# Keeping DMA transposes, accumulating DMAs and GpSimd pieces apart in a list-scheduled attention kernel

## Chip, cores, metric

One core of one Trainium2 chip. The metric is the device time of one execution in microseconds (us). Every execution of the kernels that is used here was in the fast state; three of before's (858.6, 858.9 and 860.4 us) were in the slow one and are left out. The single run of the measuring program m1 has no state. Each execution also comes with the mean clock that TensorE was granted, as a share of full speed; that number turns out to matter.

## The reference, cut to what matters

```python
# S = 2048, D = 512, H = 32 heads, Dh = 16; bf16 inputs
g = sigmoid((x * gate_w).sum(-1, keepdims=True))
a = softmax(q @ k.T * Dh**-0.5) @ v           # per head, then @ wo        (branch A)
phi(t) = concat(softmax(t @ w_phi), softmax(-t @ w_phi))                 # (branch B)
b = phi(q) @ (phi(k).T @ v) / (phi(q) @ phi(k).sum(s) + 1e-6)            # then @ wo
return g * a + (1 - g) * b
```

Branch A costs 32 x 2048 x 2048 exponentials. They are the bulk of the work.

## The kernel before

A Python program lists all operations with their dependencies. A list scheduler simulates the engines with assumed durations and fixes the order of every engine's instructions; `place` then turns dependencies and buffer reuse into semaphore waits. So a number in the scheduler ("plan value") changes the order on the chip, and an assumed duration that is wrong makes the chip's timing drift from the plan.

The parts that matter here, in short:

- TensorE computes scores into PSUM, ScalarE takes the exponential (832 operations of 128x1024), TensorE multiplies by V.
- 96 score tiles get their exponential from VectorE and GpSimd instead. VectorE converts scores to integers (EW). GpSimd, sometimes VectorE, splits them into a fraction Ef and an exponent ED. VectorE evaluates a polynomial (Em, then Ef again). Then GpSimd issues an **accumulating DMA** ED += Ef, and a TensorE matmul reads ED.
- Branch B needs **DMA transposes** issued by SyncE: 48 of phi (128x1024) and 16 of the output (128x512).
- TensorE's busy time contains matmuls that only add zeros (`ps_ot<-zero,iden`: 110.0 us in before, 121.1 us in after). The scheduler puts them where its plan leaves TensorE idle, so a wait that the plan did not foresee has none of them.

```python
# 96 times: the accumulating DMA and its reader
v = s.op("pool", SWD[0], lambda e: e.dma_start(
    out().bitcast(dt.int16), Ef().bitcast(dt.int16), accum_op=ALU.add), [g_] + hs, pr, frees=[ef], dma=SWD[1])
v.kind = "acc"
...
return s.op("pe", 0.2155, ..., deps=vs + [self.o_V[(kt, part)]], ..., frees=[ed])

# 48 times: the transpose of phi
ev = self.s.op("sp", 1.3, lambda e: e.dma_start_transpose(
    self.phiT[:, pt.idx], self.phi[:, ph.idx].rearrange("p h s f -> p (h s f)")), deps, prio,
    alloc=[pt], frees=frees, dma=1)
ev.lat = 2.6
ev.kind = "phi"

# Sched.run: the port that VectorE and GpSimd share, and the landing of a DMA, as the plan saw them
if o.port:
    other = "dve" if e == "pool" else "pool"
    now = max(now, hold[other])
    hold[e] = now + o.dur
...
if o.dma > 1:
    dma_t = max(dma_t, o.end) + o.dma / 250e3
    o.end = dma_t + o.lat
else:
    o.end += o.lat
```

The plan models the shared port but does not enforce it; it knows nothing of two DMAs slowing each other.

The softmax here doesn't subtract the row's maximum and nothing guards it: scores larger than these inputs give would overflow.

Of the kernel before, what the change touches and what calls it, by code (L numbers as in the profile page):

```python
# [31 lines left out]
LEAD = [30.0, 5.0, 15.587634343078882, 18.596008015614277, 21.376333972175523, 40.540151693083416, 4.700229106743385, 13.0]  # L32
PACE = [0.942023613127232, 0.45790104673263465]
BOUNDS = [3.0710501327799653, 8.000889564597248, 8.0295624987611, 18.02257936663145, 29.86797202712817]
# [4 lines left out]
AFF = [4.15497164884861, 0.18343314021531576, 3.4899946808590343, 0.0, 0.0, 2.90437474412157, 0.0, 3.2417994652524023, 0.0, 0.04936235801504704, 0.5936669881661917, 0.48380220117050143, 0.0, 3.63018746007737, 3.491920909382754, 0.0, 2.1406325166983535, 0.0, 0.21204954920410735, 2.3328020332964208, 0.0, 0.22787943080925754, 0.0, 0.0, 0.7354200939583246, 0.0, 0.0, 0.0, 3.722000841705053, 0.0, 0.0, 0.0, 0.0]  # L39
PAIR = [0] * 33  # L40
JOINT = [0, 0, 1, 1, 1, 1, 0, 0, 0, 1, 0, 0, 1, 1, 0, 0, 0, 0, 0, 0, 1, 0, 0, 1, 0, 0, 0, 0, 0, 0, 1, 0, 0]
SWD = [0.65, 662500, 1.85]
OFF = [0.0, -0.8897703043510494, 0.5172481291637241, -1.6001482920023302, 2.691800625687394, -4.61876105583856, 9.931835604720934, 3.749480399812751, -2.5354011754586376, 6.457003779301287, 7.051784018513548, -6.13598057955875, 6.241188808437798, -6.3176738336357, -4.720084637924602, 5.808771137792029, 1.4939627059612288, 11.762173704833385, -7.056266514883313, 1.602535412833622, -2.1339281934554815, 6.8960641134545035, -1.5364304379614095, -4.520043988488846, -1.9086060678527623, 4.191789611328016, 0.0, -10.92683283831524, 7.908073056639142, -2.846662271061698, 1.1690496888958446, 2.378092297094616, 0.0]
PRI = [-2.5977761809841518, 12.575398704445774, 3.895376356683779, 7.787259417549168, -8.651933190709245, 8.964622677949125, 0.4457880973056989, 12.368950578623885, 19.409552720225648, -3.2493945476953874, -5.057883055897609, 4.784017942556362, 8.536057932420114, 2.626494246393886, 12.999207097537264, -0.8374814899478146, -17.665801839387232, -7.161052481135956, -12.903739516547825, 10.87669422388445, 2.941617488397717, -4.250877620548464, 10.157188453890655, -20.005512559792166, -9.773812266304459, 1.8583573414742158, -5.94449476159381, -2.8717857218875027, -7.6958394115627495, -2.7824756511447886, -12.357333215935258, 8.557379841186394, 0.0]
SHY = [0.9001243968886534, 1.4809346778702634, 0.0, 1.4435036371133614, 0.2648245103916662, 0.9580856445374635, 0.0, 0.0, 0.6445455027631356, 0.7309428588090539, 1.1375351044326518, 2.3433455863822243, 0.7756902927692249, 0.0, 0.5, 1.1003534700919317, 3.2731939951157525, 0.6932697202707927, 0.0, 1.9277987030895938, 0.6784790768552428, 0.0, 0.8699058379080198, 0.16347116433726255, 0.7631355271096165, 0.1372776832486249, 1.130856988716154, 3.243248686223888, 0.0, 0.5743497984785182, 0.26482053971962666, 0.0, 0.5]
FILL = [0.5, 0.8711172814468358, 0.09241059669762763, 0.6175020065897155, 0.5968855613401888, -0.08603643695579696, 0.35836419719938023, 0.5586945605907905, 0.5, 0.21748892677719284, 0.45750545023833894, 0.5973287974855181, 0.8575217902838435, 0.3303883794680146, 0.23663805939196605, -0.05074327763890446, 0.2084505307424424, 0.7627302738218456, 0.02798645175032277, 0.6920770580745201, 0.07174908565670901, 0.784881042335597, 0.9386617589290094, 0.3031481489097715, 0.2677360487923325, 0.24925630002968974, 0.3016740589041108, -0.013731781829222231, 0.4009774331892926, 0.4360673208434442, 0.33279011555474275, 0.6155190493677356, 0.5]
SLIP = [0.007477558429250707, 0.013771949294956619, 0.06040700872331797, 0.005290126503821307, 0.0, 0.04422179282875663, 0.0, 0.0, 0.0, 0.07161288987940874, 0.0, 0.0, 0.004963247503648168, 0.03943355056146375, 0.0, 0.002957841477534724, 0.0, 0.0, 0.06406254955060428, 0.009649379279412312, 0.06237810720540699, 0.07310479040093273, 0.037191229424563266, 0.03425975512431642, 0.0, 0.0924937571943965, 0.02436668932101764, 0.015526190087033388, 0.0417233434314886, 0.0764626104914441, 0.12735071923751323, 0.12964507975379921, 0.0]
POLY = [2.5698857428809108, -0.7915744377372271, 3.711634300285815, 3.2368110322825703, -2.325206997995846, 5.4861275628456045, -1.2275371530929335, 2.3718927004339707, 2.3718927004339707, 6.413096867619973, 5.17610762451314, -0.08970465716275755, 4.7841112088256725, 2.774473851459849, -2.7397699965795126, 1.9545390919678927, -1.3153066215108966, 1.617483163920298, 6.204660286247156, 5.766200947445682, 4.7687278506630655, -3.064800512746859, 7.929141786271487, 0.22420426790201642, 2.5526418134024933, 2.3718927004339707, -4.71404655949348, -1.3350112925734097, -2.638697537980217, -1.2887908683802543, 5.121320728096021, 2.3718927004339707, 2.3718927004339707]
SHAPE = [0, 1, 2, 2, 2, 1, 1, 2, 2, 2, 0, 0, 0, 1, 2, 0, 2, 0, 0, 0, 1, 1, 1, 0, 1, 0, 1, 1, 1, 1, 1, 1, 1]
# [11 lines left out]
DVE_COUNT = (1, 3, 3, 3, 3, 3, 3, 3, 1, 3, 4, 3, 3, 3, 3, 3, 3, 3, 4, 2, 4, 3, 3, 3, 3, 3, 4, 3, 4, 3, 3, 3)  # L61
# [22 lines left out]
class BufPool:  # L84
    def __init__(self, n):
        self.free = [(0.0, i, ()) for i in range(n)]
        self.parked = []
        self.want = None

# [32 lines left out]
class Sched:  # L122
# [18 lines left out]
    def op(self, eng, dur, fns, deps=(), prio=0.0, rel=0.0, alloc=(), frees=(), dma=0, order=(),  # L141
           cols=0, cfg="F", port=False, gate=False, alt=0.0):
        if not isinstance(fns, (list, tuple)):
            fns = [fns]
        if eng == "pe" and not cols:
            cols = 90
        o = Op(eng, dur, list(fns), deps, prio, rel, alloc, frees, dma, order, cols, cfg, port, gate, alt)
        if eng == "dve" and any(getattr(b.pool, "scarce", False) for b in o.frees):
            o.prio -= LEAD[2]
        self.ops.append(o)  # L150
        return o
# [34 lines left out]
    def run(self):  # L186
# [6 lines left out]
        t = {e: 0.75 for e in self.ENGS}  # L193
# [3 lines left out]
        out = []  # L197
        cfg = "F"
        hold = {"dve": 0.0, "pool": 0.0}
        parked, last = [], None  # L200
        self.at = 0
# [26 lines left out]
        while left:  # L228
# [43 lines left out]
            held, o = [], None  # L272
# [46 lines left out]
            for it in held:  # L319
                heapq.heappush(ready[e], it)  # L320
            ok = True
            for b in o.alloc:
                if b.idx is not None:
                    continue
                pool = b.pool
                pool.free.sort()
                need = sum(x.pool is pool and x.idx is None for x in o.alloc)
                w = pool.want
                if len(pool.free) < need or (
                        w is not None and w is not o and w.start is None and w.prio < o.prio):  # L330
                    pool.parked.append(o)
                    ok = False
                elif pool.free[need - 1][0] > now:
                    push(o, pool.free[need - 1][0])
                    ok = False
                if not ok:
                    if need > 1:
                        pool.want = o
                    break
# [10 lines left out]
            if o.port:  # L350
                other = "dve" if e == "pool" else "pool"
                now = max(now, hold[other])
                hold[e] = now + o.dur
            if e == "dve":
# [30 lines left out]
            if o.dma:  # L385
# [5 lines left out]
            out.append(o)  # L391
            left -= 1
# [20 lines left out]
    def place(self, nc, ctx):  # L413
# [12 lines left out]
        sems = {e: ctx.enter_context(nc.semaphore(f"c_{e}")) for e in self.ENGS if e != "sp"}  # L426
# [41 lines left out]
class _Kernel:  # L468
# [504 lines left out]
    def dve_pack(self, n, kt, first_pv):  # L973
# [31 lines left out]
        for x in range(0, 4, 2 if PAIR[n] else 1):  # L1005
            pq = pr if x == 0 or not CHAIN else -2e3 + pr
            if PAIR[n]:
                bs = [self.bank(1), self.bank(1)]
                lo = lambda bs=bs: (min(b.idx for b in bs), max(b.idx for b in bs))
                bank = [lambda k=k, lo=lo: self.ps_mp[:, lo()[k], :] for k in range(2)]  # L1010
# [3 lines left out]
                ws += [conv(x, 2, lambda lo=lo: self.ps_mp[:, lo()[0]:lo()[1] + 1:lo()[1] - lo()[0], :], m, 1.134, bs)] * 2  # L1014
# [351 lines left out]
```

## Time and profile before

| | before |
|---|---|
| time, median of 4 runs with the comparison | 849.2 us (847.5 to 853.1) |
| profiled execution | 847.1 us, its span 845.3 us, mean clock 0.990 |
| ScalarE between first and last exponential | 828.0 us, of which 28.0 idle in 45 stretches |
| transposes issued less than 3 us after an accumulating DMA | 23 of 64 |
| VectorE Em<-Ef, 128x2048 | 1319 ns mean |

How to read the views: in a timeline, a line is start, duration, engine, source line, operation, and in brackets the idle time just before and what ended it. A row of windows gives busy time by engine, then the granted clock of TensorE ("PEclk"), the DMA share and GB/s. The main readings stand in the prediction.

One view the prediction did not take, and which I read only when all runs were done: the same execution cut at the edges of the stretches in which TensorE ran at half clock. Busy windows of before, three times the stretch ahead and the stretch itself:

```profile
core 0: us, PE busy (x) PEld busy (x) DVE busy (x) ACT busy (x) POOL busy (x), PEclk, DMA share, GB/s
297.15:300.57 3.41, 1.37 (x11) 0.29 (x8) 3.41 (x4) 1.63 (x3) 1.42 (x2) 1.00 0.70 138
300.57:303.98 3.41, 3.41 (x16) 0.69 (x12) 2.83 (x5) 2.10 (x3) 1.05 (x1) 0.50 0.19 38
321.05:324.46 3.41, 0.00 (x0) 0.00 (x0) 2.22 (x3) 0.32 (x1) 0.89 (x1) 1.00 0.47 92
324.46:327.87 3.41, 2.79 (x22) 0.48 (x22) 2.81 (x4) 0.75 (x1) 0.00 (x0) 0.50 0.53 104
112.83:116.25 3.41, 2.29 (x23) 0.77 (x20) 3.01 (x7) 2.85 (x4) 2.96 (x4) 1.00 0.31 64
116.25:119.66 3.41, 3.08 (x19) 0.56 (x18) 2.44 (x6) 2.81 (x5) 1.86 (x3) 0.50 0.59 116
```

A stretch of 3.41 us in which TensorE had little to do (1.37 and 0.00 us busy) is followed by one at clock 0.50. The third pair shows that busy time alone gives no sharp limit: TensorE was busy 2.29 us and half clock followed. The half-clock records of an execution lie on one grid of 3.41 us. Cutting the thirteen kept traces of these kernels on their grids (without the first 6 and the last 8 us), all 24 windows at full clock with TensorE busy below 1.8 us were followed by half clock, 11 of 55 from 1.8 to 2.3 us, and 1 of 3010 above. Between first and last exponential there are 17.1 us at half clock in this execution (five units of 3.41 us: from 116.2, 300.6, 324.5, and two from 471.2), and 9.3 of ScalarE's 28.0 idle us lie inside them. So a long stall can be paid twice: once as itself, and again in the stretch at half clock that follows. The pair of after and a0 below shows this once.

### The profile page before, as it was taken

To read this page: it belongs to the slowest core of one execution; us is meant where nothing else is said; L and a number is where in the kernel's file an instruction comes from. 1 tells how busy PE (TensorE), PEld (TensorE's weight loads), DVE (VectorE), ACT (ScalarE), POOL (GpSimd) and SP (SyncE) were. 2 spreads that over 40 slices of the span, in tenths; PEclk is the share of its full clock that TensorE was granted. 3 is DMA by queue.
4 is the path that set the end of the run, shared out by engine and by line. 5 is a ranking of instruction groups with operands and counts; after the bars stand their busy time and mean duration, and the time that the engine had idled before them with its cause. 6 is when DMAs were issued, how large, how long until landed. Compare 5 with 4: busy or idle time off the path is not lost.

```text
span 845.3 us, 15301 instructions
## 1 busy us (share of the span) xinstructions
PE 764.4 (90%) x6053; PEld 237.3 (28%) x6134; DVE 783.3 (93%) x1141; ACT 804.1 (95%) x904; POOL 443.2 (52%) x553
## 2 busy tenths in 40 slices
PE   8999999999998887988999698989988989998898
PEld 3333323233333222222222222222222222222222
DVE  7989989999899997999999699999999999999994
ACT  6999999999999987999999699999999999999997
POOL 2358636765364533445556154554545456855552
PEclk9999999999999999999999899999999999999999
DMA  6443554554454445445354445443545353433343
GB/s 132 108 93 76 94 100 82 82 101 84 84 121 87 83 82 84 85 91 110 78 106 93 71 85 113 86 86 78 113 79 110 66 103 69 97 67 78 78 94 81
DMA packets 96743, 76.39 MB, mean 90 GB/s; under 512 B 76832, under 2 KB 84384, under 8 KB 96672
## 3 DMA queue, kind: packets, MB, share of 16 engines
q0 software_dynamic: 13824, 50.34, 31.3%
q1 hardware_dynamic: 81504, 24.55, 14.4%
q8 instruction: 48, 0.79, 0.4%
q10 hardware_dynamic: 1344, 0.52, 0.3%
q14 instruction: 23, 0.19, 0.1%
HBM read 3.69 MB, written 2.10 MB: 7 GB/s over the span
## 4 chain that ended last, share of the span: by engine, by line
ACT 61%; DVE 15%; PE 12%; DMA 9%; issue 1%; POOL 1%; SPq 1%
ACT ET L906 59%; DMA phiT<-phi 4%; PE ps_ring L888 4%; DVE EW L1000 4%; DMA ED<-Ef 3%; DVE Em L1038 3%; ACT phi L1197 2%; DVE Ef L1042 2%; PE ps_ot L945 2%; PE ps_mp L729 1%; DVE Em L1040 1%; DVE Ef L1029 1%; DMA qT<-qst 1%; PE ps_mp L1275 1%; PE ps_mp L995 1%
## 5 line engine op out<-in xcount | busy, mean ns | idle before, releaser
L906 ACT ACTIVATE ET<-ps_ring 128x1024 bf16<-128x1024 f32 x832 | 776.2, 1133 | 29.9 <-PE ps_ring L888 28.9
L888 PE MATMUL ps_ring<-qT,kT 64*128 64x512 bf16 x1664 | 329.2, 389 | 38.7 <-ACT ET L906 22.8
L1033 POOL TENSOR_SCALAR ED<-EW 128x512 int16<-128x512 int16 (+1 forms) x326 | 257.6, 832 | 194.7 <-DVE Ef L1042 66.9
L1000 DVE TENSOR_SCALAR EW<-ps_mp 128x512 int32<-128x512 f32 x384 | 243.8, 679 | 22.1 <-PE ps_mp L995 17.3
L1029 POOL TENSOR_SCALAR Ef<-EW 128x1024 f16<-128x1024 uint16 (+1 forms) x123 | 108.5, 882 | 111.7 <-DVE Ef L1042 34.4
L888 PEld LDWEIGHTS ps_ring<-qT,kT 64*128 64x128 bf16 x1664 | 80.0, 93 | 298.7 <-ACT ET L906 263.0
L945 PE MATMUL ps_ot<-ET,Vaug 128*17 128x512 bf16 x1664 | 152.6, 387 | 0.3 <-DVE T L1085 0.3
L1045 POOL DMA_DIRECT2D ED<-Ef x96 | 87.3, 909 | 82.2 <-DVE Ef L1042 68.6
L1038 DVE TENSOR_TENSOR Em<-Ef 128x2048 f16<-128x2048 f16 x96 | 126.6, 1319 | 0.5
L995 PE MATMUL ps_mp<-qT,kT 64*128 64x512 bf16 (+1 forms) x348 | 113.7, 381 | 12.3 <-DVE EW L1000 6.3
L1042 DVE TENSOR_TENSOR Ef<-Ef,Em 128x2048 int16<-128x2048 f16 x96 | 122.1, 1272 | 0.5
L964 PE MATMUL ps_ot<-zero,iden 128*32 128x512 bf16 (+2 forms) x568 | 110.0, 378 | 0.0
L1029 DVE TENSOR_SCALAR Ef<-EW 128x1024 f16<-128x1024 uint16 (+1 forms) x113 | 76.1, 684 | 1.8 <-DMA ED<-Ef 1.8
L1040 DVE TENSOR_SCALAR Em<-Em 128x2048 f16<-128x2048 f16 x96 | 68.8, 716 | 0.3
L945 PEld LDWEIGHTS ps_ot<-ET,Vaug 128*17 128x17 bf16 x1664 | 34.8, 87 | 84.1 <-issue 78.0
L995 PEld LDWEIGHTS ps_mp<-qT,kT 64*128 64x128 bf16 (+1 forms) x384 | 33.8, 95 | 54.2 <-DVE EW L1000 25.0
L1056 PE MATMUL ps_ot<-ED,Vaug 128*17 128x512 bf16 x384 | 38.2, 388 | 8.1 <-DMA ED<-Ef 7.8
L729 PE MATMUL ps_mp<-xT,WA 128*128 128x512 bf16 (+1 forms) x119 | 37.5, 381 | 3.1 <-DVE EW L1000 1.5
L729 PE MATMUL ps_mp<-Wp,xT 128*128 128x512 bf16 x114 | 38.4, 390 | 1.2 <-issue 0.8
L964 PEld LDWEIGHTS ps_ot<-zero,iden 128*32 128x32 bf16 (+2 forms) x573 | 34.1, 94 | 17.6
L1210 DVE TENSOR_TENSOR phi<-phi,ps_mp 128x1024 bf16<-128x1024 bf16 x32 | 38.5, 1207 | 0.3
L1197 ACT ACTIVATE phi<-ps_mp 128x512 bf16<-128x512 f32 x64 | 38.2, 709 | 0.0
(90 smaller groups left out, 397.2 us busy)
## 6 DMA issues: line engine op xcount, KB each, us to landing
ED<-Ef POOLq DMA_DIRECT2D x96, 512.0 KB, 4.7
qT<-qst SPq DMA_DIRECT2D x120, 16.0 KB, 1.8
out_dram<-outt SPq DMA_DIRECT2D x12, 128.0 KB, 1.8
WA<-in_A_wqkv_dram SPq DMA_DIRECT2D x3, 384.0 KB, 4.5
phiT<-phi SPq DMA_TRANSPOSE x48, 3.4
WBV<-in_B_wqkv_dram SPq DMA_DIRECT2D x1, 512.0 KB, 7.2
Wp<-in_A_wo_dram SPq DMA_DIRECT2D x1, 512.0 KB, 3.5
WBV<-in_B_wo_dram SPq DMA_DIRECT2D x1, 512.0 KB, 4.5
```

Source lines behind the costliest of these rows:

```text
L729: m = s.op("pe", self.c_mm(n), lambda e, c=c: e.matmul(self.bk(b)[:, 0:n], lhs(c), rhs(c), start=(c == 0), stop=(c == 3)), deps if c == 0 ...
L888: return lambda e: e.matmul(self.ps_ring[:, x % RING, :], self.kT[r, g // 2, kt * P:(kt + 1) * P], self.qT[r, n % 2, i, :], start=True, st ...
L906: self.o_exp.append(s.op("act", w * 0.434 + 0.039, lambda e, b0=b0, s0=s0, w=w: e.activation(self.ET[:, s0:s0 + w, :], self.ps_ring[:, b0: ...
L945: return lambda e: e.matmul(self.ps_ot[32 * i:32 * i + VSL, :], self.Vaug[:, kt, h, :], self.ET[:, (4 * p + k) % NSLOT, :], start=(kt == 0 ...
L964: return lambda e: e.matmul(self.ps_ot[c:c + nc, :], self.iden[r:r + nr, 0:nc], self.zero[r:r + nr, :], start=False, stop=False, tile_posi ...
L995: return lambda e: e.matmul(bank(), self.kT[r, cp, kt * P:(kt + 1) * P], self.qT[r, n % 2, i, :], start=True, stop=True, tile_position=(r. ...
L1000: return s.op("dve", dur, lambda e: e.tensor_scalar(self.EW[:, ew.idx, x * QCH:(x + w) * QCH].rearrange("p (b q) -> p b q", b=w) if w > 1 else
L1029: fs = [s.op("pool", U * 8.26e-4 + 0.28, lambda e, c=c: e.tensor_scalar(self.Ef[:, ef.idx, U * c:U * c + U], half(0, dt.uint16, c, U), flo ...
L1033: hs = [s.op("pool", W * 8.26e-4 + 0.165, lambda e, c=c: e.tensor_scalar(self.ED[:, ed.idx, W * c:W * c + W].bitcast(dt.int16), half(1, dt ...
L1038: u = s.op("dve", 1.13, lambda e: e.tensor_tensor(self.Em[:], Ef(), Ef(), ALU.mult), fs + [self.ed_prev], pr, port=True)
L1042: g_ = s.op("dve", 1.13, lambda e: e.tensor_tensor(Ef().bitcast(dt.int16), Ef(), self.Em[:], ALU.mult), [q], pr, port=True)
L1045: v = s.op("pool", SWD[0], lambda e: e.dma_start(out().bitcast(dt.int16), Ef().bitcast(dt.int16), accum_op=ALU.add), [g_] + hs, pr, frees= ...
```

## The change

Intent: keep apart what hurts each other. Five parts:

1. A transpose that the plan would issue within 3 us after an accumulating DMA waits for that DMA's landing; an accumulating DMA planned within 1.2 us after a transpose waits for a mark (a no-operation) that SyncE sets behind the transpose's issue.
2. Landing times in the plan are per kind and depend on neighbours.
3. A GpSimd piece planned within 0.97 us of an accumulating DMA's issue, while VectorE holds the shared port, waits for that VectorE operation.
4. Paired score tiles need two adjacent PSUM banks.
5. Many plan values are new. The text below calls them searched; the record shows the new values, not how they were found.

```diff
+CLEAR = [3.0, 1.2, 0.97]
-PAIR = [0] * 33
+PAIR = [1, 0, 0, ... 1, 1, 1, 0, 0, 1, 1, 1, 0, 1, 1, 1, 0, 0]
-OFF = [0.0, -0.8897703043510494, ...      # likewise LEAD, PACE, BOUNDS, AFF, JOINT, PRI, SHY,
+OFF = [0.0, -0.8897703043510494, ...      # FILL, SLIP, POLY, SHAPE, DVE_COUNT (cut)
@@ Sched.run
+            near = [a for a in accs if now - a.start < CLEAR[0]] if o.kind in ("phi", "onT") else ()
+            if near:
+                o.war.append(near[-1])
+                push(o, self.seen(near[-1]))
+                continue
@@
             if o.port:
                 other = "dve" if e == "pool" else "pool"
+                if e == "pool" and accs and now < accs[-1].start + CLEAR[2] and hold["dve"] > now:
+                    if holder not in o.war:
+                        o.war.append(holder)
+                        push(o, self.seen(holder) + 0.03)
+                        continue
                 now = max(now, hold[other])
                 hold[e] = now + o.dur
+                if e == "dve":
+                    holder = o
+            if o.kind == "acc" and mark is not None and now < mark.end + CLEAR[1]:
+                o.war.append(mark)
+                now = max(now, self.seen(mark) + 0.05)
@@
+            if o.kind:
+                if o.kind == "acc":
+                    o.end = max([o.start + (5.5 if turns and o.start - turns[-1] < 1.3 else 4.7)] +
+                                [a.end + 2.65 for a in accs[-1:]])
+                    accs.append(o)
+                else:
+                    o.end = o.start + (4.15 if o.kind == "qT" else 3.05 if o.kind == "phi" else 2.43)
+                    ...                                   # later still beside an unfinished acc (cut)
+                    if o.kind != "qT":
+                        turns.append(o.start)
+                        mark = Op("sp", 0.06, [lambda e: e.nop()], (), 0.0, 0.0, (), (), 0, ())
+                        ...
+                        tail = mark
@@ place
-        sems = {e: ctx.enter_context(nc.semaphore(f"c_{e}")) for e in self.ENGS if e != "sp"}
+        sems = {e: ctx.enter_context(nc.semaphore(f"c_{e}")) for e in self.ENGS}
@@ dve_pack: two adjacent banks for a pair
-                lo = lambda bs=bs: (min(b.idx for b in bs), max(b.idx for b in bs))
+                lo = lambda bs=bs: min(b.idx for b in bs)
```

## The prediction

> **What bounds the kernel now.** I read the page's first part, then busy time by stretch, then ScalarE's waits, and last the timeline around the longest of them.
>
> ```profile
> span 845.3 us, 15301 instructions
> PE 764.4 (90%) x6053; PEld 237.3 (28%) x6134; DVE 783.3 (93%) x1141; ACT 804.1 (95%) x904; POOL 443.2 (52%) x553
> ...
> L906 ACT ACTIVATE ET<-ps_ring 128x1024 bf16<-128x1024 f32 x832 | 776.2, 1133 | 29.9 <-PE ps_ring L888 28.9
> ```
> ```profile
> 0.00:10.00 10.00, 7.58 (x47) 3.98 (x47) 6.51 (x17) 2.16 (x3) 3.12 (x8) 1.00 0.74 157
> 10.00:838.00 828.00, 752.66 (x5989) 231.77 (x6067) 774.00 (x1117) 799.92 (x898) 440.13 (x545) 0.99 0.46 90
> 838.00:846.00 8.00, 4.11 (x20) 1.51 (x20) 2.83 (x9) 2.06 (x4) 0.00 (x0) 1.00 0.20 66
> ```
>
> ScalarE's exponentials are the work that sets the end (832 of them, 776.2/832 = 0.933 us each). From 10 to 838 us ScalarE is busy 799.92 of 828 us (fourth pair in the row), so it is idle 28 us. The 10 us ahead of the first exponential and the 7 us after the last are loads and output, which the change does not touch. So the whole prize is those 28 us: with none left the span would be 845.3 - 28 = 817.3 us (-3.3%).
>
> The timeline of ScalarE gives each idle stretch its place. Two are far larger than all others. The first, with the two DMA issues that precede it and TensorE's wait:
>
> ```profile
> 314.55 0.88 POOL L1045 DMA_DIRECT2D ED<-Ef  x1
> 314.61 1.24 SPq L1216 DMA_TRANSPOSE phiT<-phi  x1
> ```
> ```profile
> 325.08 0.61 PE L1056 MATMUL ps_ot<-ED,Vaug 128*17 128x512 bf16 x4 [5.05 <-DMA ED<-Ef]
> ```
> ```profile
> 327.12 1.02 ACT L906 ACTIVATE ET<-ps_ring 128x1024 bf16<-128x1024 f32 x1 [5.76 <-PE ps_ring L888]
> ```
>
> An accumulating DMA (GpSimd) and a DMA transpose (SyncE) are issued 0.06 us apart. Both land after 10.5 us. TensorE, which runs in order, stands at the matmul that reads ED, the score matmuls behind it don't run, and ScalarE starves for 5.76 us. At 463.4 us the same happens again (issues 0.07 us apart, 10.2 and 10.3 us to landing, 5.50 us idle). Nothing else comes near these landings, as the views of the two tiles show (ED first, then phiT):
>
> ```profile
> DMA to landing us min/median/max: 4.4/4.7/10.5
> ```
> ```profile
> DMA to landing us min/median/max: 3.0/3.4/10.6
> ```
>
> The second pattern is GpSimd's next piece right behind its DMA issue, here VectorE and then GpSimd:
>
> ```profile
> 288.10 2.79 DVE L1038 TENSOR_TENSOR Em<-Ef 128x2048 f16<-128x2048 f16 x1
> ...
> 296.44 2.69 DVE L1029 TENSOR_SCALAR Ef<-EW 128x1024 f16<-128x1024 uint16 x1
> ```
> ```profile
> 287.83 0.88 POOL L1045 DMA_DIRECT2D ED<-Ef  x1
> 288.44 1.37 POOL L1033 TENSOR_SCALAR ED<-EW 128x1024 int16<-128x1024 int16 x1
> ```
>
> VectorE's 288.10 operation takes 2.79 us where its undisturbed peers take 1.2, and its 296.44 operation 2.69 where peers take 0.68. Both ran beside a GpSimd piece that followed a DMA issue. ScalarE then idles 0.89, 0.42, 1.78, 0.40 and 0.91 us between 292 and 304 us.
>
> Sorting all of ScalarE's idle stretches by what TensorE stood at just before gives this **ledger** of the 28 us:
> - A, the two double landings with the short stalls that follow them (0.24; 0.64 and 0.43): 5.76 + 5.50 + 1.31 = 12.6.
> - B, GpSimd behind a DMA issue holding VectorE up: 4.40 (292 to 304), 0.78 (418), 1.01 (511 to 515), 0.48 (555 to 558) = 6.7.
> - C, TensorE waiting for other landings (phiT at 166, 446, 568, 675; ED at 115 with what follows, 360, 364; qT at 263, 628): 6.2.
> - D, the rest: 2.5.
>
> **What the Trainium skill says.** "SBUF — State Buffer", section "Who interferes with whom": VectorE and GpSimd share a port pair as an exclusive lock, and whichever comes first blocks the other for its whole instruction. The trace agrees: VectorE's 1.2 us operation grew to 2.79 beside a GpSimd piece. The same page, section "SBUF: two separate sides", has a VectorE operation starving GpSimd's descriptor writing. Here it is rather VectorE that loses: GpSimd's issue keeps 0.88 us while VectorE stretches. "DMA: Bandwidth & Descriptors", section "Rules for kernel authors", says a transpose next to ordinary DMAs needs nothing. That is about correct data; for time the trace disagrees (3.05 us alone, 10.6 when issued together with an accumulating one). No section I read explains the 10.5 us.
>
> **The change part by part.** The work stays: I compared the instruction order of both programs. ScalarE has the same 832 + 64 large activations, and there are 96 accumulating DMAs and 64 transposes (48 phiT, 16 onT) in both.
>
> 1. Transposes against accumulating DMAs. In the new order 17 of 64 transposes wait for an accumulating DMA's landing (none before), and 26 of 96 accumulating DMAs wait for a mark that SyncE sets after a transpose's issue (none before). This is a real wait on both sides, so an issue 0.06 us apart should not occur where the plan sees the two near each other. Removes A: -12.6. What it costs: a transpose issued within 3 us after an accumulating DMA landed in 5.51 us on average before (18 of them). Held to that DMA's landing it needs what is left of 4.7 us (some 3 us as an estimate for an issue in the middle of the 3 us) and then 3.05, so about 6: no real loss, and no gain in latency. An accumulating DMA loses up to about 1.2 us when it waits for a mark. Both sit off the path where the order leaves room. SyncE gets 64 extra short instructions, 0.06 us each by the code's own figure, about 4 us on an engine with long pauses: hidden.
>
> 2. The scheduler's landing times are now per kind and depend on neighbours, so TensorE's readers are placed later when a landing will be late. That should help C. I take half: -3.1.
>
> 3. GpSimd pieces next to a DMA issue. Of the 96 pieces that follow a DMA issue, 65 waited for VectorE before, 89 do now. Removes part of B; the rule only holds where the plan has VectorE busy on the shared port, and drift of the real order defeats some. I take 60%: -4.0. GpSimd is 52% busy, so its own waiting costs nothing directly.
>
> 4. New plan values. 58 evictions of 128x1024 replace 116 of 128x512. From the VectorE groups, 128x128 takes 283 ns and 128x512 takes 679, so 1.03 ns a column and 1024 columns about 1207 ns (estimate). Pairs of the small ones take 1.27 to 1.29 us in the timeline, so 0.07 us is saved each, 58 x 0.07 = 4 us. Against that VectorE takes over 7 more 1024-wide and 3 more 512-wide Ef pieces (7 x 0.67 + 3 x 0.41 = 6 us). GpSimd loses 84 + 19 pieces of 0.62 us and gains 42 + 1 of 1.05: 64 - 45 = 19 us less. So VectorE stays about as loaded (+2 us of 783) and neither becomes the bound. The paired score matmuls need two adjacent banks of three, which can make TensorE wait.
>
> 5. A new order brings new small stalls, which nobody can read from the old trace. The 43 new DMA waits and the pairs are likely sources; I put +4 us, of the size of two thirds of C.
>
> Sum: -12.6 - 3.1 - 4.0 + 4 = -15.7. From 849.1 that gives 833.4; I say **833 us** (-1.9%).
>
> **The rivals.**
> - *The stall is moved, not removed.* Held transposes land late, phiT has two buffers only, and its readers stall TensorE as before; SyncE issues in order, so a held transpose also delays the qT copies behind it. For it: phiT already stands at 4% in the chain that ended last, and qT ended a 1.1 us stall. Against it: TensorE's readers are re-placed by the same scheduler that holds the transpose. It would give back 6 to 8 us: about 841.
> - *VectorE becomes the bound.* It is 93% busy and its overlong operations cost it some 12 us near DMA issues. If waiting pieces are pushed into its other port operations, or shifted pieces and bank pairs crowd it, the end follows VectorE: 840 to 845. Against it: the load changes by 2 us only.
> - *Nearly all stalls go.* A, B and C share one cause, events that the old plan did not see. If the new plan is right in most of them, 22 of 28 us go and new ones are few: about 825.
>
> **Range and chances.** A is almost certain (I see the 10 us landings gone with 9 in 10), so the middle lies between -10 and -20 us. The rivals put the ends at 823 and 843. The 2% line is at 849.1 x 0.98 = 832.2, right beside my number; runs of before scatter from 847.5 to 853, and a fast baseline in the comparison makes 2% harder. Faster by over 2%: 0.42. Within 2%: 0.56. Slower by over 2%: 0.02, since new waits would have to cost 30 us.
>
> **What would show it.** Right: the largest landing of ED and phiT near 7 us or less; no ScalarE wait over 2 us between 10 and 838 us; ScalarE busy still 804 us, so its idle time there down to some 12 us; VectorE's Em<-Ef mean down from 1319 ns towards 1220, its busy time between 775 and 790. Wrong: landings near 10 us still there (the waits miss the pairs that collide); or landings fine and ScalarE still idle over 20 us, with TensorE standing at phiT, qT or EW instead; or ScalarE idle near zero.

## The result, and the profile after

**823.8 us** (median of 4 runs, 821.8 to 825.4) against 849.2 for before in the same comparison: ratio 0.9694, 95% interval 0.9654 to 0.9734, faster by 3.1%. A ratio here is the mean time of one kernel's fast runs over that of the other's in the same rounds, so not quite the ratio of the medians. The predicted 833 missed by 9 us, inside the range and at its lower end.

The page of after, its first part and ScalarE's main group:

```profile
span 823.6 us, 15309 instructions
PE 772.6 (94%) x6131; PEld 235.6 (29%) x6131; DVE 775.6 (94%) x1093; ACT 801.8 (97%) x904; POOL 414.9 (50%) x493
...
L950 ACT ACTIVATE ET<-ps_ring 128x1024 bf16<-128x1024 f32 x832 | 774.4, 1152 | 10.3 <-PE ps_ring L932 9.9
```

The last column of the group is what ScalarE waited before exponentials: 10.3 us where it was 29.9. Busy windows of after:

```profile
10.00:816.00 806.00, 761.73 (x6061) 230.56 (x6062) 766.32 (x1068) 797.58 (x898) 411.80 (x485) 1.00 0.47 92
816.00:824.00 8.00, 4.06 (x24) 1.33 (x22) 2.82 (x9) 2.06 (x4) 0.00 (x0) 1.00 0.20 66
```

ScalarE is idle 8.4 us of the 806.0 (before 28.1 of 828.0) and busy 2.3 us less. The two make the 22.0 us by which the stretch is shorter (from first to last exponential exactly it is 21.8: 19.6 of idle and 2.2 of busy time). The tile views of ED and of phiT in after:

```profile
DMA to landing us min/median/max: 4.4/4.5/6.1
```
```profile
DMA to landing us min/median/max: 3.0/3.1/4.8
```

Both double landings (10.5 and 10.6 us before) are gone, and the counts fit: no transpose is issued within 3 us after an accumulating DMA any more (23 before). The longest ScalarE stall left, in the timeline of after, with the TensorE matmul ahead of it:

```profile
384.30 1.03 PE L1039 MATMUL ps_mp<-qT,kT 64*128 64x512 bf16 x3 [1.32 <-DMA qT<-qst]
...
385.80 1.02 ACT L950 ACTIVATE ET<-ps_ring 128x1024 bf16<-128x1024 f32 x1 [1.43 <-PE ps_ring L932]
```

TensorE waits 1.32 us for a qT copy. The new waits themselves show as GpSimd waiting for SyncE's marks (waits of GpSimd in after: total us, times, longest):

```profile
POOL ED L1089 <- SPq L422: 34.0, 16, 4.5
```

34 us of waiting in 16 waits (2.1 us each, the longest 4.5), all on an engine that is busy 50%. VectorE's groups, first in before, then in after:

```profile
L1038 DVE TENSOR_TENSOR Em<-Ef 128x2048 f16<-128x2048 f16 x96 | 126.6, 1319 | 0.5
```
```profile
L1082 DVE TENSOR_TENSOR Em<-Ef 128x2048 f16<-128x2048 f16 x96 | 122.3, 1274 | 0.6 <-POOL Ef L1073 0.2
...
L1044 DVE TENSOR_SCALAR EW<-ps_mp 128x1024 int32<-128x1024 f32 x58 | 70.6, 1217 | 5.2 <-PE ps_mp L1039 4.7
```

### The profile page after: what moved, and what is told of

Its sections match the earlier page's. It is cut to its first block, busy times and chain, and to the rows that moved or that the text cites. A ratio compares the mean times of both kernels' runs of the same rounds, so it can differ in the third digit from the quotient of the medians.

```text
span 823.6 us, 15309 instructions
## 1 busy us (share of the span) xinstructions
PE 772.6 (94%) x6131; PEld 235.6 (29%) x6131; DVE 775.6 (94%) x1093; ACT 801.8 (97%) x904; POOL 414.9 (50%) x493
## 4 chain that ended last, share of the span: by engine, by line
ACT 67%; PE 13%; DVE 11%; DMA 6%; SPq 1%; issue 1%; POOL 0%; ACTq 0%
ACT ET L950 65%; PE ps_ring L932 4%; DVE EW L1044 3%; DMA ED<-Ef 3%; ACT phi L1241 2%; PE ps_ot L989 2%; PE ps_mp L773 2%; DVE Ef L1086 2%; PE ps_mp L1039 1%; DVE Em L1082 1%; DMA qT<-qst 1%; PE ps_mp L1319 1%; DMA phiT<-phi 1%; DVE Em L1084 1%; DVE phi L1254 1%
## 5 line engine op out<-in xcount | busy, mean ns | idle before, releaser
L950 ACT ACTIVATE ET<-ps_ring 128x1024 bf16<-128x1024 f32 x832 | 774.4, 1152 | 10.3 <-PE ps_ring L932 9.9
L1077 POOL TENSOR_SCALAR ED<-EW 128x512 int16<-128x512 int16 (+1 forms) x284 | 235.2, 855 | 171.8 <-DVE Em L1082 57.6
L1044 DVE TENSOR_SCALAR EW<-ps_mp 128x512 int32<-128x512 f32 (+1 forms) x326 | 241.6, 777 | 19.2 <-PE ps_mp L1039 14.8
L1073 POOL TENSOR_SCALAR Ef<-EW 128x1024 f16<-128x1024 uint16 (+1 forms) x105 | 95.2, 907 | 109.0 <-DVE Ef L1086 37.9
L989 PE MATMUL ps_ot<-ET,Vaug 128*17 128x512 bf16 x1664 | 147.3, 384 | 0.2 <-DVE T L1129 0.2
L1082 DVE TENSOR_TENSOR Em<-Ef 128x2048 f16<-128x2048 f16 x96 | 122.3, 1274 | 0.6 <-POOL Ef L1073 0.2
L1008 PE MATMUL ps_ot<-zero,iden 64*128 64x512 bf16 (+2 forms) x570 | 121.1, 380 | 0.0
L1084 DVE TENSOR_SCALAR Em<-Em 128x2048 f16<-128x2048 f16 x96 | 71.5, 745 | 0.1
L1039 PEld LDWEIGHTS ps_mp<-qT,kT 64*128 64x128 bf16 (+1 forms) x384 | 29.8, 94 | 49.0 <-DVE EW L1044 19.9
L773 PE MATMUL ps_mp<-Wp,xT 128*128 128x512 bf16 x128 | 41.2, 384 | 0.1
L1008 PEld LDWEIGHTS ps_ot<-zero,iden 64*128 64x128 bf16 (+2 forms) x570 | 36.0, 94 | 17.6 <-issue 0.2
```

The costliest lines, as they stand in the source:

```text
L773: m = s.op("pe", self.c_mm(n), lambda e, c=c: e.matmul(self.bk(b)[:, 0:n], lhs(c), rhs(c), start=(c == 0), stop=(c == 3)), deps if c == 0 ...
L950: self.o_exp.append(s.op("act", w * 0.434 + 0.039, lambda e, b0=b0, s0=s0, w=w: e.activation(self.ET[:, s0:s0 + w, :], self.ps_ring[:, b0: ...
L989: return lambda e: e.matmul(self.ps_ot[32 * i:32 * i + VSL, :], self.Vaug[:, kt, h, :], self.ET[:, (4 * p + k) % NSLOT, :], start=(kt == 0 ...
L1008: return lambda e: e.matmul(self.ps_ot[c:c + nc, :], self.iden[r:r + nr, 0:nc], self.zero[r:r + nr, :], start=False, stop=False, tile_posi ...
L1039: return lambda e: e.matmul(bank(), self.kT[r, cp, kt * P:(kt + 1) * P], self.qT[r, n % 2, i, :], start=True, stop=True, tile_position=(r. ...
L1044: return s.op("dve", dur, lambda e: e.tensor_scalar(self.EW[:, ew.idx, x * QCH:(x + w) * QCH].rearrange("p (b q) -> p b q", b=w) if w > 1 else
```

## The experiments

Two kinds of experiment are used. In a **same-order** run every engine's instruction order was checked to be that of after (or before), and only waits differ. In a **re-planned** run the scheduler was given another rule or value and produced another order. The second kind turned out to say little, which the control e8 shows.

Runs of one session share before's runs: session 1 (e1 to e4, chip 3) has before at 851.8 us median of its fast runs, session 2 (m1, e5, e7, e8, chip 10) 850.7, session 3 (e9 to e11, a0, chip 10) 855.2. By the rule that calls 2% a difference, a0, e2, e9 and e11 are faster than before, e1, e3, e4 and e8 the same, and e5, e7 and e10 unclear; smaller differences are read from the intervals.

| run | what | us (range) | ratio to before (95%) |
|---|---|---|---|
| a0 | after again | 824.9 (822.4 to 825.3) | 0.966 (0.961 to 0.971) |
| e4 | before's order + 2 waits between DMAs | 838.3 (832.6 to 840.6) | 0.985 (0.982 to 0.989) |
| e11 | e4 + 5 waits of GpSimd pieces | 828.8 (828.6 to 829.6) | 0.971 (0.965 to 0.977) |
| e1 | after without the 43 DMA waits | 840.6 (838.9 to 841.7) | 0.987 (0.984 to 0.991) |
| e2 | after without the pieces' waits | 826.0 (823.4 to 830.8) | 0.971 (0.967 to 0.976) |
| e3 | after without both | 839.5 (837.5 to 848.7) | 0.988 (0.983 to 0.994) |
| e9 | after without the 17 waits of transposes | 831.4 (828.6 to 834.0) | 0.974 (0.969 to 0.980) |
| e10 | after without the 26 waits for marks | 840.0 (833.8 to 844.3) | 0.984 (0.976 to 0.991) |
| e5 | new rules, old values (re-planned) | 866.6 (861.2 to 868.9) | 1.019 (1.012 to 1.026) |
| e7 | rule 3 off in the plan (re-planned) | 863.8 (861.2 to 866.3) | 1.016 (1.008 to 1.024) |
| e8 | one value changed by 0.5% (re-planned) | 852.3 (848.2 to 855.7) | 1.002 (0.999 to 1.004) |

### e4: only the two collisions, in the old order

Before's order with two waits: the two accumulating DMAs of ledger A wait for a mark behind the transpose that had been issued with them.

```diff
@@ place, before
+        for k, m in ((30, 26), (48, 41)):
+            a, t = accs[k], turns[m]
+            mark = Op("sp", 0.06, [lambda e: e.nop()], (), 0.0, 0.0, (), (), 0, ())
+            ...                                  # put behind t on SyncE
+            a.war.append(mark)
```

> The kernel before, same order on every engine, with just two waits more: the two accumulating DMAs that were issued 0.06 us ahead of a transpose now wait until SyncE has issued that transpose (some 1.3 us later). Ledger item A: both 10 us landings go (5 to 6.5 us instead), ScalarE's idle time falls by 11 to 12.6 us, the time is 836.5 to 839 us. Rival 'given back later': another wait (VectorE's EW, the other landings) takes the place of most of it, 843 to 847 us.

Measured: 838.3 us, ratio 0.9853. 1.47% of some 851 us is 12.5 us for two waits. The timeline of e4 at the place of the first collision:

```profile
310.46 1.24 SPq L1230 DMA_TRANSPOSE phiT<-phi  x1
...
312.05 0.88 POOL L1059 DMA_DIRECT2D ED<-Ef  x1 [1.61 <-SPq L420]
```

The transpose goes first and GpSimd waits 1.61 us for the mark. The two landings are 3.06 and 4.4 us where they were 10.6 and 10.5. In the profile ScalarE's idle time between exponentials falls from 28.0 to 14.7 us. What follows: ledger A (12.6 us) is right in place, cause and size, half clock included (clock 0.989 to 0.998 in e4's six executions, 0.977 to 0.992 in the fast ones of before beside them). Whether the two need the rest of the kernel's traffic is what m1 tests.

### m1: the collision by itself

A program of its own (its output is zeros, wrong on purpose): 156 trials of one 512 KB DMA from GpSimd and one transpose from SyncE, the second released by a ScalarE operation of stepped length after the first, with nothing else running.

```python
for k, (kind, add, first, n) in enumerate(TRIALS):      # GpSimd; SyncE and ScalarE likewise
    e.wait_ge(s_pool, k + 1)
    e.dma_start(ED[:], Ef[:], accum_op=ALU.add) if add else e.dma_start(ED[:], Ef[:])
```

> A small program of its own (its result is zeros, wrong on purpose): the same accumulating DMA of 512 KB from GpSimd and the same transpose from SyncE, again and again, nothing else running, with the time between the two issues stepped from about -3 to +3 us; then the smaller onT transpose, then the 512 KB DMA without accumulation. Theory 'two issues within 0.1 us of each other block each other': landings of 9 to 11 us for both at offsets of 0 to +0.1 us, 5 to 6 us at larger ones, 4.4 and 3.05 us alone. Rival 'the 10 us need the rest of the kernel's traffic' (qT copies, busy ports): no landing over 7 us at any offset. If the accumulation matters, the plain DMA shows no such peak.

Measured, phi transpose and accumulating DMA (offset is the transpose's issue minus the DMA's issue, landing is from each one's own issue):

| offset, us | accumulating DMA lands after | transpose lands after |
|---|---|---|
| alone | 4.5 | 3.04 |
| -1.43 | 4.50 | 3.04 |
| -0.60 | 5.2 to 5.35 | 3.05 |
| -0.07 | 5.9 | 5.7 |
| -0.015 | 6.6 | 6.65 |
| +0.012 | 8.3 to 9.2 | 8.3 to 9.2 |
| +0.04 | 10.2 | 10.0 |
| +0.065 | 10.5 to 10.65 | 10.3 to 10.4 |
| +0.09 | 8.2 to 8.6 | 8.4 to 8.8 |
| +0.145 | 5.6 | 6.1 |
| +1.1 | 4.95 | 5.05 |
| +1.96 | 4.8 | 4.0 |

The tile views of m1 for ED, phiT and onT, over all its trials:

```profile
DMA to landing us min/median/max: 2.8/4.8/10.6
```
```profile
DMA to landing us min/median/max: 3.0/4.0/10.4
```
```profile
DMA to landing us min/median/max: 2.4/3.2/5.5
```

The 128x512 transpose has no peak (at most 5.5 us, 2.4 alone), and the phi transpose beside a plain DMA of the same 512 KB has none either (at most 4.7 for the plain one, 5.1 for the transpose). So the pair alone is enough; the kernel's other traffic is not needed. And two things are told apart. From an offset of about -1 us to +2 us the two slow each other by 0.3 to 3 us (the transpose only from about -0.5 us on). On top of it the large transpose and the *accumulating* DMA double in a window about 0.1 us wide. Why that window exists stays open: these runs give its shape, not its cause.

### e1, e2, e3: after with its waits taken out, same order

```diff
@@ e1 (e3: both parts)
             if near:
-                o.war.append(near[-1])
                 push(o, self.seen(near[-1]))
@@
             if o.kind == "acc" and mark is not None and now < mark.end + CLEAR[1]:
-                o.war.append(mark)
                 now = max(now, self.seen(mark) + 0.05)
@@ e2 (e3: both parts)
-                    if holder not in o.war:
-                        o.war.append(holder)
+                    if holder not in o.gone:      # a list that place() does not read
+                        o.gone.append(holder)
```

The plan still counts with the waits, so the order stays; only the semaphores are gone.

> The changed kernel, every engine's order exactly as in it, but without the 17 waits of transposes for an accumulating DMA and the 26 waits of accumulating DMAs for SyncE's mark (the marks are still set). Theory 'the semaphores do it': the engines drift, transposes and accumulating DMAs meet again within 0.1 us, some landings near 10 us come back, and the time is 830 to 838 us. Rival 'the new order does it': the order already keeps them apart, landings stay under 7 us, and the time stays within 3 us of 823.8.

> The changed kernel, same order on every engine, but without the waits of GpSimd pieces for VectorE that the new rule adds (85 instead of 89 of the 96 pieces behind a DMA issue still wait for VectorE for other reasons). Theory 'these waits protect VectorE': some Em<-Ef operations again take 2.5 us and more, and the time is 826 to 830 us. Rival 'the order did it' (only 4 pieces differ): 822 to 826 us and Em<-Ef mean at 1270 ns within 20.

> The changed kernel, same order, with both kinds of added waits taken out. Theory 'the semaphores do it': the sum of the two losses, 832 to 842 us. Rival 'the new order does it': within 4 us of 823.8.

Measured: e1 840.6 us, e3 839.5, e2 826.0. The 43 DMA waits together are worth some 16 us in the new order (840.6 - 823.8 = 16.8 by medians, 1.8% by ratios). The landings near 10 us that were expected did not come back in e1's profile: they reach only 6.9 (ED) and 7.2 us (phiT). Seven phi transposes and one of the output came within 0.4 us of an accumulating DMA. Three of them (offsets +0.39, -0.12 and -0.08 us, landing after 5.7, 5.8 and 7.2 us) stand ahead of its longest ScalarE stalls, which begin at 91, 268 and 395 us. So the waits pay also by preventing the milder slowing.

Removing the waits of GpSimd pieces (e2) makes no difference in time that can be resolved (823.4 to 830.8 us). It is a weak test: only 4 pieces lose their last wait on VectorE (85 instead of 89 of 96 wait, the rest are held by other waits anyway). Its profile does show some protection lost: one Em<-Ef takes 3.12 us where the longest in after takes 2.07, and the mean is 1296 ns where it was 1274. So the theory and its rival each came true in part. What rule 3 does for the time, if anything, comes through the order or through waits that stay. e3 is e1 within the scatter.

### e9 and e10: which of the two kinds of DMA wait

```diff
@@ e9: transposes no longer wait
-                o.war.append(near[-1])
@@ e10: accumulating DMAs no longer wait for marks
-                o.war.append(mark)
```

> The changed kernel, same order on every engine, without the 17 waits of transposes for an accumulating DMA's landing; the 26 waits of accumulating DMAs for a mark stay. Removing all 43 cost some 15 us. If the held transposes carry it (transposes issued 0.1 to 3 us behind an accumulating DMA land after 4 to 6 us where the order counts on 3): 832 to 840 us. If the marks carry it: 823 to 828 us.

> The counterpart: the changed kernel, same order, without the 26 waits of accumulating DMAs for a mark behind a transpose's issue; the 17 waits of transposes stay. If the marks carry it (an accumulating DMA slips ahead of a transpose into the window of 0 to 0.1 us or close before it): 832 to 840 us. If the held transposes carry it: 823 to 828 us. If both are needed, each of the two kernels loses 5 to 10 us.

Measured beside a0 (824.9): e9 831.4, so +6.5 us; e10 840.0, so +15 us. They are not additive: without both it is +16. e9 fell just below the range for held transposes; e10 is at the upper end of the range for marks; that each loses 5 to 10 us came true for e9 alone. The timelines of each show one collision. e9, the accumulating DMA and the stall that follows (its transpose was issued 0.10 us behind it; landings 11.0 and 11.3 us):

```profile
559.31 0.88 POOL L1088 DMA_DIRECT2D ED<-Ef  x1 [2.81 <-SPq L421]
...
572.10 1.02 ACT L949 ACTIVATE ET<-ps_ring 128x1024 bf16<-128x1024 f32 x1 [6.08 <-PE ps_ring L931]
```

e10, where the DMA slips to 0.07 us behind the transpose (landings 9.9 and 10.1 us):

```profile
389.28 1.31 SPq L1259 DMA_TRANSPOSE phiT<-phi  x1
389.35 0.87 POOL L1088 DMA_DIRECT2D ED<-Ef  x1
...
400.20 1.02 ACT L949 ACTIVATE ET<-ps_ring 128x1024 bf16<-128x1024 f32 x1 [6.52 <-PE ps_ring L931]
```

So both halves are needed: in these profiles either alone leaves one collision that costs ScalarE over 6 us in one piece. e10 has the milder slowing of e1 besides (ScalarE idle 4.4 us between 90 and 96 us, behind a transpose that was issued 0.38 us after an accumulating DMA and landed after 5.7 us), and e9 does not. In the kernel the window also holds at -0.07 and at +0.10, a little wider than in m1 (5.9 us at -0.07, 8.2 to 8.6 at +0.09); at -0.08, in e1, the landings were 6.9 and 7.2 us.

### e11: GpSimd pieces held, in the old order

e4 plus five waits: five GpSimd pieces that had stretched a VectorE operation right after a DMA issue wait for that operation.

```diff
@@ place, before (with e4's part)
+        for d, p in ((411, 207), (420, 210), (577, 275), (700, 326), (760, 353)):
+            d, p = D[d], Q[p]            # d-th VectorE, p-th GpSimd operation
+            ...
+            p.war.append(d)
```

> The kernel before, same order on every engine, with the two DMA waits of the earlier run (which gave 0.985) and five more: at the five places where VectorE was stretched to 1.5 to 3.5 us by the GpSimd piece behind a DMA issue, and ScalarE then stalled, that piece now waits for the VectorE operation. Ledger item B, right: those operations back near 1.2 and 0.7 us, ScalarE's idle time 5 to 7 us less, 0.976 to 0.980 of before (about 831 to 834 us of 851). Rival 'the stall is only moved' (GpSimd's later piece delays the next DMA): 0.983 to 0.988, as without the five waits.

Measured: 828.8 us, ratio 0.9714, against 838.3 and 0.9853 for e4: 9.6 us by medians for five waits, more than expected (the two come from different sessions and chips; the ratios differ by 1.4%). The profiled executions differ by less, 4.0 us of span, as e4's was its fastest (832.6 us). In them the stalls at ledger B's places, 4.6 us in e4, are gone in e11, while a stall at phiT has grown from 0.8 to 2.9 us with what follows it. The timeline of e11 at the place that the prediction showed at 287.83 and 288.10:

```profile
285.88 0.88 POOL L1071 DMA_DIRECT2D ED<-Ef  x1
...
286.15 1.21 DVE L1064 TENSOR_TENSOR Em<-Ef 128x2048 f16<-128x2048 f16 x1
...
287.46 1.04 POOL L1059 TENSOR_SCALAR ED<-EW 128x1024 int16<-128x1024 int16 x1 [0.70 <-DVE Em L1064]
```

The same VectorE operation takes 1.21 us instead of 2.79, because the piece now starts 0.1 us after its end. The other four went from 2.69, 2.71, 3.54 and 2.49 us to 0.83, 1.22, 1.21 and 1.21. Across the kernel, VectorE's group in e11:

```profile
L1064 DVE TENSOR_TENSOR Em<-Ef 128x2048 f16<-128x2048 f16 x96 | 120.1, 1252 | 0.5
```

So **seven waits in the old order give 828.8 us**, most of what the whole change gives (824.9 in the same session, intervals overlapping).

### e5, e7, e8: re-planned, and a control

```diff
@@ e5: new rules, before's plan values for all lists
@@ e7
-CLEAR = [3.0, 1.2, 0.97]
+CLEAR = [3.0, 1.2, 0.0]
@@ e8
-LEAD = [..., 21.09664890476773, ...]
+LEAD = [..., 21.2, ...]
```

> The changed code with the plan values of the kernel before (27 of 64 transposes wait for an accumulating DMA, 24 accumulating DMAs for a mark). Theory 'code alone': waits and landing times take items A and half of C away, whatever the values: 830 to 838 us. Rival 'the values carry a large part': an order not tuned for the new rules gives back much in new stalls, 838 to 850 us.

> The changed kernel with the rule for GpSimd pieces next to a DMA issue taken out of the planning too (65 of 96 pieces behind an issue wait for VectorE, not 89; the order moves with it). Theory 'the rule, as a planning rule, removed item B': Em<-Ef mean back above 1300 ns, several operations over 2.4 us, and 828 to 834 us. Rival 'B went with the new values': Em<-Ef mean below 1290 ns, 823 to 828 us.

> A control: the changed kernel with one plan value moved by half a per cent (the lead time of the qT copies, 21.097 to 21.2), which means nothing but gives a different order. It tells how much an order not searched for costs. If orders are interchangeable: 822 to 827 us. If the search behind the values matters: 827 to 836 us, with small stalls at phiT, qT or ED.

Measured: e5 866.6, e7 863.8, e8 852.3 us. In none of the three did the time come out as expected. e8 keeps every rule, moves one value by half a per cent and loses 28 us. In its profile ScalarE is idle 26.8 us between the exponentials, and one wait at the tail has grown from 3.0 to 10.9 us. The collisions are gone in all three (landings of ED at most 6.7 us in e5, 6.6 in e7 and e8).

Most of what came instead was in the plans. The scheduler needs no chip: run again from each run's kernel.py when this text was checked, it plans an end at 803.2 us for before, 804.1 for after, and 829.0, 826.0 and 821.4 for e5, e7 and e8. So these three plans are 17 to 25 us longer than after's before any drift. e8's plan has both of its large stalls: 5.8 us between exponentials (5.96 in the trace, at 715.7 us, where TensorE runs 60 of the zero matmuls) and 12.1 us ahead of the output (10.9 in the trace).

What follows: one changed value (e8) costs 28 us, more than any rule here, and some 17 of them could have been read from the plan. e5 and e7 lose 43 and 40 us, but as they are re-planned orders too, they can't say what the old values or the missing rule cost on the chip. The reverse pairing, old rules with the new values, was not run: without the new bank code the check ahead of the chip refuses the program for a conflict of TensorE and VectorE in a PSUM bank.

### a0: the yardstick

> The changed kernel itself once more, as the yardstick on this chip for the runs beside it: 822 to 827 us, 0.967 to 0.973 of before.

After again: 824.9 us, ratio 0.966, like the first time. Its profile is a stroke of luck. It has the same qT stall as the first profile of after, but no half clock. Busy windows of the first execution of after around the stall:

```profile
380.64:384.05 3.41, 1.70 (x14) 0.40 (x14) 2.53 (x5) 3.41 (x5) 2.00 (x3) 1.00 0.81 56
384.05:387.47 3.41, 3.17 (x20) 0.78 (x21) 1.89 (x3) 1.38 (x3) 0.47 (x1) 0.50 0.95 191
387.47:390.88 3.41, 3.41 (x20) 1.08 (x18) 2.01 (x3) 2.60 (x3) 0.94 (x1) 0.50 0.00 0
```

and of a0:

```profile
379.70:383.10 3.40, 2.41 (x20) 0.59 (x20) 3.40 (x5) 3.40 (x6) 1.96 (x3) 1.00 0.82 61
383.10:386.50 3.40, 2.09 (x23) 0.80 (x24) 1.65 (x3) 2.52 (x4) 1.37 (x2) 1.00 0.86 173
386.50:389.90 3.40, 3.40 (x29) 1.05 (x28) 3.40 (x7) 3.40 (x5) 1.29 (x2) 1.00 0.11 20
```

The same program and the same TensorE wait for qT (1.32 and 1.29 us). In the first the stall lies in one 3.41 us window, which leaves TensorE busy 1.70 us; the next two run at clock 0.50 and ScalarE is idle 2.03 + 0.81 = 2.8 us in them. In a0 the edges cut the stall in two (2.41 and 2.09 us busy), no half clock follows, and ScalarE loses 0.88 us. The edges in a0 are carried back in steps of 3.413 us from its only half-clock record, at 820.03 us, behind the last exponential. The spans are 823.6 and 820.6 us.

## Why the prediction was right, and where its sizes were off

The direction held, and so did the mechanism of the largest term, A. B's mechanism was shown in the old order; C's gain did not appear. The sum was 9 us too cautious by medians, 6 in the profiled pair:

| term | predicted | profile | shown by |
|---|---|---|---|
| A, double landings | -12.6 | -12.6 | e4 -12.5 us; e1, e9, e10 bring collisions or slow landings back |
| B, VectorE held up | -4.0 | -6.7 | e11, 9.6 us of medians, 4.0 of profiled spans |
| C, other landings, and new stalls | -3.1 + 4 | +0.2 (6.2 to 6.4) | after's timeline |
| D, the rest | 0 | -0.5 (2.5 to 2.0) | after's timeline |
| ScalarE busy | 0 | -2.2 | windows of both |
| sum | -15.7 | -21.8 | spans 845.3 and 823.6 |

**A was right** in cause, place and size. That the new waits cost nothing directly fits too: 34 us of GpSimd waiting for marks sit on an engine with half its time free. But their size was wrong: a wait was put at up to about 1.2 us, and the 16 took 2.1 on average and 4.5 at most.

**B was mis-sized by my choice of 60%.** I reasoned that drift would defeat some of the waits. In after none of ledger B's stalls is left. What e11 shows is that held pieces can remove all of B's stalls when they are the right ones. That after's gain comes from such waits is not shown: e2 took the last wait from only 4 pieces and lost no time that can be resolved. How much of B after gets from the rule and how much from the new order is not separated.

**C did not fall by half.** It is 6.2 us before and about 6.4 after: four ED landings of 1.96 us in sum, two qT copies with follow-ups of 3.65, one phiT of 0.76. So the better landing model shows no gain of its own here. The +4 us for new stalls was counted on top of what was left of C; in fact what is left *is* the new stalls. Together they were expected at 3.1 + 4 = 7.1 us and came to 6.4, so the total was nearly right, with a wrong split.

**ScalarE's busy time was taken as fixed.** It fell by 2.2 us with the same work. A restart costs: a lone exponential takes 1.02 us, one in a train 0.92 (10 in 9.17 us), and there are 25 idle stretches instead of 45, so about 20 x 0.10 = 2 us.

**The term that was missing: the half clock.** Of the 28 us I sorted by cause, 9.3 lay inside windows at half clock. The stalls at 300 to 304, which I gave to VectorE alone, lie in such a window (ScalarE 2.10 of 3.41 us busy). The clock also goes with the scatter of before, and so with the fact that the medians moved by 25.3 us while the profiled pair moved by 21.7. In the 38 fast executions of before in the three later sessions, the time runs from 844.8 us (clock 0.990) to 857.9 (clock 0.974), with a correlation of -0.93 and a slope of 7.0 us for each 0.01 of clock. One window of 3.41 us at half clock takes 0.0020 off the mean, so it goes with about 1.4 us. The profiled execution of before had 5 such windows; a median one of those 38, at 852 us and 0.982, has (1 - 0.982) x 850 / 0.5 = 31 us, so about 9. The eight executions of after have clock 0.996 to 1.000: none to two windows (the four at 1.000 average 823.0 us, the four at 0.996 or 0.997 825.1). By this slope 0.006 of clock, some 4 us of the gain, are tied to half clock in the profiled pair (0.990 to 0.996), and 0.012 to 0.014, some 9 to 10 us, between typical ones (849 to 851 us lie at 0.986 to 0.984 on that line, and the eight of after average 0.998). These are estimates, and they are not on top of A, B and C but the echo of them. In a correlation stall and half clock come together; only the pair of after and a0 shows the half clock apart from the stall, once.

**Rivals.** "The stall is moved" fell: ScalarE's longest stall between exponentials is 1.43 us. "VectorE becomes the bound" fell: its busy time is 775.6 us, inside the 775 to 790 that I named. "Nearly all stalls go", about 825 us, is what happened; it deserved more than an end of the range. Only C, which it counted among the stalls that go, kept its size.

**Readings of the prediction that the traces correct.** VectorE's load was to rise by 2 us; it fell by 7.7 (783.3 to 775.6), with fewer stretched operations. The 5.51 us for transposes close behind an accumulating DMA contain the two collisions; without them the mean is 4.9, so a held transpose at about 6 us does lose some latency. And "the trace agrees" that whichever engine comes first blocks the other is half right: the two did get in each other's way, but the VectorE operation that grew to 2.79 us had begun 0.34 us before the GpSimd piece.

**What the prediction could have looked at.** The plan itself: it ends at 803.2 us for before and 804.1 for after. The new plan is no shorter. The profiled span of before ran 42 us past its plan, that of after 19.5, so the whole gain lies in a plan that the chip follows more closely.

Still open: what makes the 0.1 us window; how often before's other executions collide, since only the profiled one was seen; how the last 4 us between e11 and after divide between rules, bank pairs and values; and what rule 3's waits are worth in after's order.

## What to carry to other kernels

Look for the few longest stalls of the bounding engine and ask which two instructions were issued together just before: here two waits recovered 12.5 us and five more 4 (profiled spans) to 10 (medians). Judge a rule inside a scheduler by adding or removing its waits in a fixed order; a re-planned order is a new draw, and one draw can cost more than the rule. Compare the plans' own lengths before the chip is used. And read the granted clock beside the time: here every window of 3.41 us that left TensorE busy for less than 1.8 us was followed by one at half clock.

## What the Trainium skill lacked or had wrong

- "DMA: Bandwidth & Descriptors", section "Rules for kernel authors", says a transpose next to ordinary DMAs needs nothing (the row is about correct data). For time this case differs: a 128x1024 transpose issued 0.01 to 0.09 us behind a 512 KB accumulating DMA makes both land after 8.2 to 10.65 us (alone 3.04 and 4.5); issued from about 1 us ahead to 2 us behind, they cost each other 0.3 to 3 us. A plain DMA of that size, or the 128x512 transpose, shows no such peak. The page says nothing of it.
- The same page, section "Anatomy of one DMA — SWDGE (gpsimd) path", fits a DMA's time as about 2.0 us plus bytes over 436e3 per us, which is 3.2 us for 512 KB. m1, within SBUF, shows 2.85 us for the plain one and 4.5 us for the accumulating one; the page gives no figure for accumulation.
- "SBUF — State Buffer", section "SBUF: two separate sides": that whichever engine comes first takes the shared port for its whole instruction does not tell all that happens around a DMA issue. VectorE's operation began 0.34 us before GpSimd's piece and still grew to 2.79 us, while the DMA issue, which began 0.27 us before it, kept its 0.88 us. With the piece held back (e11) the same operation took 1.21 us beside the same issue.
- "TensorE: Matmul & The Clock Gate", section "Part 1: The HAM clock gate", gives free-running windows of 3413 ns and half clock after an idle one. The traces agree on 3.41 us and 0.50. They add that the window need not be idle: windows with TensorE busy 1.37 and 1.70 of 3.41 us were followed by half clock, ones with 2.09 and 2.41 (a0) were not; windows with 2.02 in e11 and 2.29 in before were.
